# Last batch of a capped-attention and routed-experts kernel: gates of its second step from values times weights, and its output products moved into the rounds of the first choice

## The chip, the core and the metric

The kernel runs on one core of a Trainium2 chip. The metric is the device time of one execution in microseconds (us). TensorE (PE on the profile) multiplies, VectorE (DVE), ScalarE (ACT) and GpSimd (POOL) work on vectors, SyncE (SP) starts most transfers. TensorE's weight loads are listed as PEld.

## The reference

Attention with capped scores for 8 batches of 12 heads, 448 tokens and 64 columns a head; then a routed layer over all 3584 tokens. Every token goes to one of 8 experts, which take at most 448 tokens each, in the order of all logits from the largest down.

```python
scores = scale * np.matmul(q, k.transpose(0, 1, 3, 2))
scores = cap * np.tanh(scores / cap)
attn = softmax(scores)                 # per query
x = np.matmul(attn, v)                 # -> [3584, 768]
logits = x @ w_gate                    # [3584, 8]
for idx in np.argsort(-logits.flatten()):
    tok, e = divmod(int(idx), 8)
    if assigned[tok] < 0 and counts[e] < 448:
        assigned[tok] = e; counts[e] += 1
for e in range(8):
    out[assigned == e] = np.maximum(x[assigned == e] @ w1[e], 0) @ w2[e]
```

## The kernel before

**Attention.** The function `attention` runs 24 steps g, three for each batch b, four heads in each (two column blocks o by two halves h). A step computes seven blocks of scores (`qk(g,r)`, lines 143 to 166): products into the PSUM tile psS (two buffers), tanh on ScalarE, then exp on ScalarE for groups of blocks; the exp of a group is issued behind the next tanh. Weights stay unnormalised in tiles e. In the same step TensorE makes the output products of the step before, `avq(g-1,...)`, into two psA tiles, and VectorE copies them into xT (`av_out`, line 219) and adds the weights up (`esum`, line 169).

**Gates.** For each batch a PSUM tile misc[b] collects twelve products (`rnd`, line 229): sums over keys of every head (kind 's') and, from the finished xT and the gate weights, unnormalised gate values (kind 'g'). VectorE copies it (`logit_in`, line 245), TensorE transposes it (`logit`, line 251), VectorE divides gate by sum and adds the heads into the logits L1 (lines 266 to 271), and `on_logits` issues the proposals (lines 473 to 501). `turnsum` (lines 239 to 241, VectorE then GpSimd) and `inv` (line 242) make the reciprocals of the sums; `scale` (line 35) divides the turned outputs Y by them and `put` (line 32) writes them to the DRAM tile xs.

**The last batch.** The last step (23) would have its outputs too late for this. So the product of values and gate weights (V times gate) is made earlier: `vload` brings the values turned (step 16), `vgate` multiplies (step 18), `vback` transposes back into the table vgs (step 21, line 128). With it `vround` (line 134) gets step 23's sums and gates from the weights directly, without outputs. The logits of batch 7 are made in two parts: `logit(b,some=True)` with the first two steps' sums and gates, and `logit(b,part)` with those of step 23. After the attention loop come `rnd(b,0,8,8)`, the four value rounds with the first part between them, half of step 23's output products (`av(g,0,...)`), and five filler products (line 346). Half of the output products (`avs`), the two scalings of batch 6 (`held`) and the transposes of the six column blocks of batch 7's outputs (`xt`, lines 40 to 47) are handed on to the next stage.

**First choice.** `select` (lines 526 to 560) finds thresholds in 16 rounds, 5 + 6 + 5: compares on VectorE (line 539 or 541) and ScalarE (line 535), a count on TensorE (line 547), a pick on VectorE (line 551). After each count, at place B, `ffn_all` puts in filler products (`warm`), an output product (`avs`) or a transpose of outputs (`units`), by the lists UN and AN; ScalarE's copies go out at place A, before the next count. After six `xt` the tile xn is complete and goes to xs in one transfer (line 47). `finalise` turns the thresholds into a list of rows; `gather` (line 851) fetches 448 rows of xs in four pieces, TensorE transposes them (line 857), and the experts follow one after another to the end of the kernel, TensorE without gaps (lines 948 and 1010).

**Order.** PE, ACT, DVE and SP run exactly in the order of the program text; GpSimd too from `ffn_all` on. In each queue a waiting instruction holds those behind it.

## Time and profile before

| what | us |
|---|---|
| median of 3 runs (all) | 841.2 (840.28, 841.2, 841.3) |
| the profiled execution, as timed | 840.35 |
| its span | 838.5 |
| last exponential of attention ends | 298.3 |
| first turn of the first choice on TensorE | 308.81 |
| gather issued | 338.92 |

| engine | busy us | share |
|---|---|---|
| PE | 818.2 | 98% |
| DVE | 594.2 | 71% |
| ACT | 565.7 | 67% |
| POOL | 393.9 | 47% |

The profile is of one execution; times in its timelines count from the start of the span. A row of a timeline gives start, length, engine, line of the kernel, operation, output and inputs, how many instructions were merged into it, and in brackets the idle time of the engine before it with what ended that.

### The profile page before, as it was taken

The page shows a single profiled execution, that of the slowest core. Times are in us where ns is not written, and L with a number is a line of the kernel's source. Part 1 is how long each engine was busy: PE and PEld are TensorE (multiplying, and loading weights), DVE is VectorE, ACT ScalarE, POOL GpSimd, SP SyncE. Part 2 cuts the span into 40 slices and gives each one's busy share as a digit, 9 for nine tenths or more (in the row PEclk, how much of TensorE's full clock was granted, in tenths as well). Part 3 has the DMA queues.
Part 4 walks back from the last instruction along what each step waited for, and adds up shares of the span by engine and source line. Part 5 has one row for each costly group of instructions (what it writes and reads, how often), then busy time and mean ns, then how long its engine had stood idle before and what let it go on. Part 6 is the DMA issues. An engine that isn't in the chain of part 4 may idle for free.

```text
span 838.5 us, 16298 instructions
## 1 busy us (share of the span) xinstructions
PE 818.2 (98%) x5784; PEld 573.7 (68%) x5784; DVE 594.2 (71%) x1914; ACT 565.7 (67%) x747; POOL 393.9 (47%) x585
## 2 busy tenths in 40 slices
PE   7999999999999988999999999999999999999997
PEld 3333333333333336688888888888888899999997
DVE  2667899989989978877878878868768874353210
ACT  7999999999999945481683684655755845544510
POOL 7600000000000033393395695686686777887843
PEclk9999999999999999999999999999999999999999
DMA  6424364654635205733566967976968958959714
GB/s 242 132 90 133 110 166 130 191 137 155 195 110 155 52 16 133 256 112 128 183 189 217 269 212 233 312 240 196 304 214 221 309 188 236 337 189 267 241 66 131
DMA packets 115859, 155.09 MB, mean 185 GB/s; under 512 B 66818, under 2 KB 80354, under 8 KB 115778
## 3 DMA queue, kind: packets, MB, share of 16 engines
q1 hardware_dynamic: 108208, 124.73, 49.3%
q0 software_dynamic: 4832, 22.03, 7.8%
q10 hardware_dynamic: 2738, 7.31, 2.3%
q8 instruction: 45, 0.74, 0.4%
q14 instruction: 36, 0.29, 0.1%
HBM read 105.18 MB, written 40.60 MB: 174 GB/s over the span
## 4 chain that ended last, share of the span: by engine, by line
PE 90%; ACT 4%; DVE 3%; issue 1%; DMA 1%; POOL 1%; SPq 0%; POOLq 0%; DVEq 0%; ACTq 0%
PE psH L948 28%; PE psH L1010 26%; PE psS L158 13%; PE psA L198 13%; PE psM L229 3%; ACT e L159 2%; ACT e L164 1%; PE psX L783 1%; PE psS L153 1%; DVE cmpD L539 1%; POOL out_dram L968 1%; PE psM L251 1%; DVE cmpD L541 1%; PE psR L547 1%; DMA on<-yb 0%
## 5 line engine op out<-in xcount | busy, mean ns | idle before, releaser
L1010 PE MATMUL psH<-hh,w2h 128*128 128x448 f32 x720 | 199.0, 367 | 0.0
L159 ACT ACTIVATE e<-psS 128x896 f32<-128x896 f32 x168 | 145.9, 916 | 13.3 <-PE psS L158 9.2
L164 ACT ACTIVATE e<-e,bias 128x1792 f32<-128x1792 f32 (+2 forms) x74 | 147.2, 1991 | 0.8
L948 PE MATMUL psH<-xgh,w1h 128*128 128x448 f32 (+1 forms) x384 | 141.8, 369 | 0.4 <-ACT xgh L898 0.2
L158 PE MATMUL psS<-tq,tk 64*64 64x448 f32 x1248 | 135.6, 543 | 5.0 <-ACT e L159 5.0
L1010 PEld LDWEIGHTS psH<-hh,w2h 128*128 128x128 f32 x720 | 134.1, 188 | 8.7 <-DVE hh L958 0.4
L948 PE MATMUL psH<-xgh,w1l 128*128 128x448 f32 (+1 forms) x384 | 139.9, 364 | 0.0
L826 POOL TENSOR_TENSOR w1l<-w1r,w1h 128x768 fp32r<-128x768 f32 x62 | 116.4, 1878 | 49.4 <-ACT w1h L819 45.1
L948 PE MATMUL psH<-xgl,w1h 128*128 128x448 f32 (+1 forms) x384 | 135.6, 366 | 0.0
L826 POOL TENSOR_TENSOR w2l<-w2r,w2h 128x768 fp32r<-128x768 f32 x64 | 132.3, 2070 | 6.0 <-ACT w2h L819 5.9
L241 POOL COPY sm<-lgt 32x84 f32<-32x84 f32 x28 | 7.0, 249 | 258.5 <-DVE lgt L239 257.7
L198 PE MATMUL psA<-e,nv 64*64 64x448 f32 x1232 | 127.7, 536 | 0.0
L1010 PE MATMUL psH<-hh,w2l 128*128 128x448 f32 x360 | 124.3, 367 | 0.0
L158 PEld LDWEIGHTS psS<-tq,tk 64*64 64x64 f32 x1248 | 42.9, 132 | 80.0 <-issue 44.8
L198 PEld LDWEIGHTS psA<-e,nv 64*64 64x64 f32 x1232 | 47.9, 133 | 67.5 <-issue 64.9
L819 ACT ACTIVATE w2h<-w2r 128x768 fp32r<-128x768 f32 x64 | 76.6, 1209 | 0.5 <-DMA w2r<-in_moe_w_dram 0.4
L948 PEld LDWEIGHTS psH<-xgh,w1h 128*128 128x128 f32 x384 | 72.4, 189 | 6.0 <-ACT xgh L898 1.3
L948 PEld LDWEIGHTS psH<-xgh,w1l 128*128 128x128 f32 x384 | 72.2, 188 | 4.5
L948 PEld LDWEIGHTS psH<-xgl,w1h 128*128 128x128 f32 x384 | 72.2, 188 | 4.4 <-DVE xgl L910 0.2
L1010 PEld LDWEIGHTS psH<-hh,w2l 128*128 128x128 f32 x360 | 67.5, 188 | 4.3
L957 ACT ACTIVATE hh<-psH 128x448 fp32r<-128x448 f32 x56 | 30.2, 539 | 57.6 <-PE psH L948 54.7
L1014 DVE STREAM_TRANSPOSE yq<-psH 128x448 f32<-128x448 f32 x45 | 35.5, 789 | 37.8 <-PE psH L1010 37.6
(400 smaller groups left out, 1285.5 us busy)
## 6 DMA issues: line engine op xcount, KB each, us to landing
w1r<-in_moe_w_dram SPq DMA_DIRECT2D x64, 384.0 KB, 4.6
w2r<-in_moe_w_dram SPq DMA_DIRECT2D x64, 384.0 KB, 5.8
nv<-in_v_dram SPq DMA_DIRECT2D x24, 448.0 KB, 5.1
tk<-in_k_dram SPq DMA_DIRECT2D x23, 448.0 KB, 3.4
tq<-in_q_dram SPq DMA_DIRECT2D x23, 448.0 KB, 4.4
yb<-yq SPq DMA_DIRECT2D x60, 168.0 KB, 3.9
xs<-Y SPq DMA_DIRECT2D x28, 336.0 KB, 5.5
on<-yb SPq DMA_DIRECT2D x7, 1152.0 KB, 7.8
```

Source lines behind the costliest of these rows:

```text
L153: for c in range(2): nc.tensor.matmul(ps[c*64:c*64+64,h,:S],tks[g,0][hp,o,u*128+c*64:u*128+c*64+64],tks[g,1][hp,o,:],start=True,stop=True)
L158: nc.tensor.matmul(ps[w:w+64,h,:S],tks[g,0][hp,o,r*64:r*64+64],tks[g,1][hp,o,:],start=True,stop=True)
L159: nc.scalar.activation(ev(g,r),ps[:,:,:S],AF.Tanh,scale=sr[0])
L164: act=lambda: nc.scalar.activation(e,e,AF.Exp,scale=sr[1],bias=bias)
L198: for h in range(2): nc.tensor.matmul(avp[g,o][h*64:h*64+64,:S],z[w,r,h,:],ev(g,r)[w,h,:],start=r==0,stop=r==6)
L229: nc.tensor.matmul(ps[k*32:k*32+32,c],lhs,rhs[:,c],start=x<4 and i==0,stop=c.stop==S and x==max(y for y in range(end) if R[y][0]==k))
L819: nc.scalar.activation(view(h),r,AF.Copy)
L826: (eng or nc.gpsimd).tensor_tensor(view(l),r,view(h).bitcast(F32),op=ALU.subtract)
L948: nc.tensor.matmul(ps[:,o:C],a[:,c,:],b[:,c,o:],start=(m==0 and o==0),stop=(m==DC*3-1)); m+=1
L957: nc.scalar.activation(h,ps[:,:C],AF.Relu)
L1010: nc.tensor.matmul(ps[:,:C],spl[p,2,hf,f//2][w][:,f%2,cc*128:cc*128+128],h[a][:,f],start=(m==0),stop=(m==nm-1))
L1014: turnq.append((now[0]+5,now[0]+(5 if p==E-1 else TL),lambda: nc.vector.transpose(yq[p][:,:,hf,cc::3],ps[:,:C])))
```

## The change

Step 22 is treated as step 23 was: its sums and gates come from values times weights as well (`vround(0,j)` within step 23, with its own tables vgs[0], wgd[0]; `vround(1,j)` is the old one). Its sums on VectorE (`esum`), its products in the loop (`avq`) and its copies (`av_out`) go. `vload`, `vgate` and `vback` run twice, at steps 10/12/13 and 15/18/19. The last step ends after its second score block and is written out: value rounds of step 22 between the score blocks, then sums and gates of batch 7's first step (`rnd(b,0,4)`), batch 6's logits, the first part of batch 7's logits between the value rounds of step 23, batch 6's `turnsum` and `inv` behind that part, its two `scale` on GpSimd and `put` behind the second copy. The output products: half of step 22's stand beside the last logits (`av(N-2,0,...)`), the other half and all of step 23's (`avlast`) go into the rounds of the first choice; the list ITEMS says for each round whether an output product ("a"), a transpose of outputs ("x") or filler is issued. The five filler products go. The PSUM pool of the outputs (psA, pT) becomes a pool psX that lives on into the experts.

```diff
-    whole=lambda g: 0<g<N-1
+    whole=lambda g: 0<g<N-2
...
-                        nc.vector.tensor_copy(vgs[w,j,2*q:2*q+2,16:24],v4[w,q].rearrange("p (h e) -> p h e",h=2))
-        def vround(j):
-            if j==0: misc[B]=pM.tile([128,512],F32,name="psM")
+                        nc.vector.tensor_copy(vgs[i][w,j,2*q:2*q+2,VW[i]:VW[i]+8],v4[w,q].rearrange("p (h e) -> p h e",h=2))
+        def vround(i,j):
+            t=misc[B-1+i]
             for o in range(2):
                 for h in range(2):
                     l=2*o+h
-                    nc.tensor.matmul(misc[B][32*l:32*l+32,:S],vgs[:,j,l,:],ev(N-1,2*j+o if j<3 else 6)[:,h,:],start=j==0,stop=j==3)
+                    nc.tensor.matmul(t[32*l:32*l+32,:S],vgs[i][:,j,l,:],ev(N-2+i,2*j+o if j<3 else 6)[:,h,:],start=j==0,stop=j==3)
...
         def esum(g,what):
-            if not 0<=g<N: return
+            if not 0<=g<N-2: return
...
+        def avlast(n):
+            g=N-1
+            avq(g,*((0,0),(1,0),(2,0),(0,1),(1,1),(2,1),(3,1))[n])
+            if n==6: return lambda: [nc.scalar.activation(xT[B-1][:,2*(g%NQ)+o,:],avp[g,o][:,:S],AF.Copy) for o in range(2)]
         def av_out(g,o):
-            if not 0<=g<N: return
+            if not 0<=g<N-2: return
...
+            elif some:
+                va=ps[:CP,:].rearrange("p (j l k) -> p j l k",j=NJ,l=4)
+                r2=xp.tile([CP,NJ,4],F32,name="rg1",bufs=1)
+                nc.vector.reciprocal(r2,va[:,:,:,16])
+                rs=xp.tile([CP,NJ,2,H//6],F32,name="rg2",bufs=1)
+                for l in range(2): nc.vector.reciprocal(rs[:,:,l,:],ps[:CP,:].rearrange("p (j s k) -> p j s k",s=8,k=16)[:,:,0::7,1+2*l])
+                t=xp.tile([CP,NJ,8,E],F32,name="lt8",bufs=1)
+                nc.vector.tensor_tensor(t[:,:,4:8,:],va[:,:,:,24:32],r2.unsqueeze(3).broadcast_to([CP,NJ,4,E]),op=ALU.mult)
+                for l in range(2):
+                    nc.vector.tensor_tensor(t[:,:,2*l:2*l+2,:],va[:,:,1+l,0:16].rearrange("p j (h e) -> p j h e",e=E),rs[:,:,l,:].unsqueeze(3).broadcast_to([CP,NJ,2,E]),op=ALU.mult)
+                nc.vector.tensor_copy(r.rearrange("p j (a h) -> p j a h",h=2)[:,:,2::2,:],r2.rearrange("p j (a h) -> p j a h",h=2))
+                nc.vector.tensor_copy(r.rearrange("p j (a h) -> p j a h",h=2)[:,:,1:4:2,:],rs)
...
-            if g==N-8: vload()
-            if g==N-6: vgate()
-            if g==N-3: vback()
+            if g==N-14: vload(0)
+            if g==N-12: vgate(0)
+            if g==N-11: vback(0)
+            if g==N-9: vload(1)
+            if g==N-6: vgate(1)
+            if g==N-5: vback(1)
...
+            if last: break
...
-        g=N-1; b=B-1
-        rnd(b,0,8,8)
+        misc[b]=pT.tile([128,512],F32,name="psX")
+        vround(0,0)
+        qk(g,2)
+        vround(0,1); vround(0,2)
+        qk(g,3); qk(g,4)
+        on_turn(bb-1)
+        rnd(bb,10,12); logit_in(bb)
+        qk(g,5); qk(g,6)
+        rnd(b,0,4)
+        vround(0,3)
+        logit(bb)
         logit_in(b)
-        turnsum(b-1)
-        vround(0); vround(1)
-        part=logit(b,some=True,pool=pT)
-        vround(2); vround(3)
+        misc[B]=pM.tile([128,512],F32,name="psM")
+        vround(1,0); vround(1,1)
+        part=logit(b,some=True)
+        turnsum(bb); inv(bb)
+        vround(1,2); vround(1,3)
         lgs[b]=xp.tile([128,S],F32,name="lg",bufs=2); ps=misc.pop(B)
         nc.vector.tensor_copy(lgs[b],ps[:,:S])
-        ps=pT.tile([128,512],F32,name="psA")
-        av(g,0,3,ps,3,2)
-        inv(b-1)
+        for i in range(2): scale(bb,i,nc.gpsimd)
+        put(bb)
+        ps=pT.tile([128,512],F32,name="psX")
+        av(N-2,0,3,ps,3,2)
         logit(b,part)
-        for j in range(3): av(g,0,j,ps,3,2)
-        ps=pT.tile([128,512],F32,name="psA")
-        for _ in range(5): nc.tensor.matmul(ps[:,:128],ident,ident,start=True,stop=True)
-    avs=[lambda ps,j=j: av(N-1,1,j,ps,0,3) for j in range(4)]
-    def held(i):
-        scale(B-2,i,nc.gpsimd)
-        if i: put(B-2)
-    return [lambda pool,i=i: lambda: held(i) for i in range(2)]+[lambda pool,p=p: xt(B-1,p,pool) for p in range(NP)],avs
+        for j in range(3): av(N-2,0,j,ps,3,2)
+        ps1=pT.tile([128,512],F32,name="psX")
+    avs=[lambda j=j: av(N-2,1,j,ps1,0,3) for j in range(4)]+[lambda n=n: avlast(n) for n in range(7)]
+    return [lambda pool,p=p: xt(B-1,p,pool) for p in range(NP)],avs
...
-    N0=1; UN=[1,0,1,0,1,0,1,0,1,1]+[0]*6; AN=(1,3,5,7)
+    ITEMS=["a","a","a","a","ax","a","x","a","a","x","a","a","x","x","x"]
...
-    units(2)
+    avs.pop(0)()
     while len(res)<1:
         step()
         if rt.pos=='B':
-            warm(2 if UN[m] else 1 if m in AN else 4)
-            if m in AN:
-                put=avs.pop(0)(pa)
-                if put: late.append(put)
-            units(UN[m%len(UN)]); m+=1
+            x=ITEMS[m] if m<len(ITEMS) else ""; m+=1
+            warm({"a":1,"x":2,"":4}.get(x,0))
+            if "a" in x:
+                copy=avs.pop(0)()
+                if copy: late.append(copy)
+            if "x" in x: units(1)
```

## Rows read from the trace of the kernel before

**Rows 1.** The page: shares of the chain that ended last, by engine.
```profile
PE 90%; ACT 4%; DVE 3%; issue 1%; DMA 1%; POOL 1%; SPq 0%; POOLq 0%; DVEq 0%; ACTq 0%
```

**Rows 2.** Timeline of ScalarE behind the value products and behind the transposition back.
```profile
225.09 1.73 ACT L159 ACTIVATE e<-psS 128x896 f32<-128x896 f32 x2 [0.71 <-PE psS L158]
227.34 0.92 ACT L159 ACTIVATE e<-psS 128x896 f32<-128x896 f32 x1 [0.53 <-PE psS L158]
...
261.56 1.73 ACT L159 ACTIVATE e<-psS 128x896 f32<-128x896 f32 x2 [0.20 <-PE psS L158]
263.81 0.92 ACT L159 ACTIVATE e<-psS 128x896 f32<-128x896 f32 x1 [0.53 <-PE psS L158]
```

**Rows 3.** Timeline of ScalarE, the last exponential of attention.
```profile
297.30 1.04 ACT L164 ACTIVATE e<-e,bias 128x896 f32<-128x896 f32 x1
```

**Rows 4.** Timeline of VectorE in the tail.
```profile
293.86 0.46 DVE L266 RECIPROCAL rin<-psM 112x48 f32<-112x48 f32 x1 [0.47 <-PE psM L251]
...
297.82 0.15 DVE L501 SCALAR_TENSOR_TENSOR r_K<-r_kk,r_Ct 112x4 f32<-112x4 f16 x1
...
300.11 0.62 DVE L245 COPY lg<-psM 128x448 f32<-128x448 f32 x1 [1.06 <-PE psM L229]
300.65 0.63 DVE L239 STREAM_TRANSPOSE lgt<-lg 128x448 f32<-128x448 f32 x1
...
303.03 0.62 DVE L277 TENSOR_REDUCE lt<-lt 112x32 f32<-112x256 f32 x1
303.84 0.62 DVE L339 COPY lg<-psM 128x448 f32<-128x448 f32 x1 [0.19 <-PE psM L134]
304.38 0.67 DVE L242 RECIPROCAL sm<-sm 128x84 f32<-128x84 f32 x1
305.29 0.26 DVE L257 RECIPROCAL rg<-psM 112x16 f32<-112x16 f32 x1 [0.24 <-PE psM L251]
...
306.61 0.19 DVE L474 TENSOR_TENSOR r_P<-L,r_m 112x32 f16<-112x32 f32 x1
...
307.58 0.19 DVE L482 TENSOR_TENSOR r_VA<-r_P,r_At 112x32 f16<-112x32 f16 x1
```

**Rows 5.** Timeline of TensorE in the tail.
```profile
302.06 1.71 PE L134 MATMUL psM<-e,vgs 128*32 128x448 f32 x16
...
307.59 1.38 PE L346 MATMUL psA<-ident 128*128 128x128 f32 x10
308.81 0.21 PE L511 MATMUL psR<-r_id,r_VA 112*128 112x112 f16 x1
```

**Rows 6.** Timelines of GpSimd and VectorE: the sums' copies, the scalings, line 652 twice.
```profile
301.41 1.11 POOL L241 COPY sm<-lgt 32x84 f32<-32x84 f32 x4 [36.78 <-DVE lgt L239]
...
309.61 4.87 POOL L35 TENSOR_TENSOR Y<-Y,sm 128x1344 f32<-128x1344 f32 x2
...
333.88 0.24 DVE L652 SCALAR_TENSOR_TENSOR gteq<-r_kk,e8s,gt 112x32 f16<-112x32 f16 x1
...
734.75 2.16 DVE L652 SCALAR_TENSOR_TENSOR gteq<-r_kk,e8s,gt 112x32 f16<-112x32 f16 x1
734.77 2.10 POOL L826 TENSOR_TENSOR w2l<-w2r,w2h 128x768 fp32r<-128x768 f32 x1
```

**Rows 7.** Timeline of TensorE: the counts of four rounds of the first choice.
```profile
320.48 0.18 PE L547 MATMUL psR<-r_cd,r_bo 128*128 128x4 bf16 x1
321.81 0.18 PE L547 MATMUL psR<-r_cd,r_bo 128*128 128x4 bf16 x1
323.12 0.18 PE L547 MATMUL psR<-r_cd,r_bo 128*128 128x4 bf16 x1
...
330.88 0.18 PE L547 MATMUL psR<-r_cd,r_bo 128*128 128x4 bf16 x1
```

**Rows 8.** Timelines (SP, GpSimd, TensorE) and, second row, the transfer's time to landing.
```profile
326.29 0.30 SPq L47 DMA_DIRECT2D xs<-xn  x1
xs<-xn SPq DMA_DIRECT2D x1, 1344.0 KB, 6.2
338.92 0.99 POOL L851 DMA_INDIRECT xg<-xs,idx  x1 [11.26 <-DVE zz L704]
344.86 0.44 PE L857 MATMUL psX<-ident,xg 128*128 128x128 f32 x2
```

More of the change, by code (lines that the diff above doesn't have):

```diff
@@ L97, in gates, with vload, vgate @@
                     nc.gpsimd.tensor_copy(gw[hp,p,c:c+8],wgs[hp,p,:])
[L98 to L104 removed]
+            for i in range(2):
+                for h in range(2): nc.gpsimd.tensor_copy(wgd[i][h*64:h*64+64,:,h*E:h*E+E],wgs[h*64:h*64+64,NP-4+2*i:NP-2+2*i,:])
+        vgs=[c2.tile([128,NJ,2*HG,32],F32,name=f"vgs{i}") for i in range(2)]
+        wgd=[c2.tile([128,2,32],F32,name=f"wgd{i}") for i in range(2)]
+        VS=(16,0); VW=(24,16)
+        for i in range(2):
+            c=VS[i]
+            nc.gpsimd.memset(vgs[i],0.0)
+            nc.gpsimd.memset(vgs[i][:,0:3,:,c:c+1],1.0)
+            for o in range(2): nc.gpsimd.memset(vgs[i][64-64*o:128-64*o,3,2*o:2*o+2,c:c+1],1.0)
+            nc.gpsimd.memset(wgd[i],0.0)
         vt={}
[L106 removed]
+        def vload(i):
             vt['t']=tp.tile([128,HG,S],F32,name="tv",bufs=1)
[L108 to L109 removed]
+            nc.sync.dma_start(vt['t'].rearrange("p m s -> p (m s)"),vl[i])
+        def vgate(i):
             ps=pM.tile([128,512],F32,name="psM"); t=vt['t']
@@ L115, in vgate, with vback @@
                         for c,u,n in [(c,u,128)] if not a*jj else [(c,u-64,128)] if o==0 else [(c,u,64),(c+64,u,64)]:
-                            nc.tensor.matmul(ps[32*k:32*k+32,c:c+n],wgd[:,o,:],t[:,o,u:u+n],start=True,stop=True)
+                            nc.tensor.matmul(ps[32*k:32*k+32,c:c+n],wgd[i][:,o,:],t[:,o,u:u+n],start=True,stop=True)
             vt['g']=xp.tile([128,256],F32,name="vg",bufs=1)
             nc.vector.tensor_copy(vt['g'],ps[:,:256])
-        def vback():
+        def vback(i):
             ps=pM.tile([128,512],F32,name="psM")
@@ L192, in avq @@
             if j==0 and x==0:
-                for o in range(2): avp[g,o]=pT.tile([128,512],F32,name="psA")
+                for o in range(2): avp[g,o]=pT.tile([128,512],F32,name="psX")
             if whole(g):
@@ L228, in rnd @@
                     else: lhs=ones[:,m,n,:]; rhs=es_t[b*NQ+m][:,n,:]
-                    nc.tensor.matmul(ps[k*32:k*32+32,c],lhs,rhs[:,c],start=x<4 and i==0,stop=c.stop==S and x==max(y for y in range(end) if R[y][0]==k))
+                    nc.tensor.matmul(ps[k*32:k*32+32,c],lhs,rhs[:,c],start=x<4 and i==0 and b<B-1,stop=b<B-1 and c.stop==S and x==max(y for y in range(end) if R[y][0]==k))
         lgs={}; lgt={}
@@ L773, in ffn_all, with warm @@
     first_rows=wp.tile([16,E],F32,name="frow",bufs=1)
-    N0=1; UN=[1,0,1,0,1,0,1,0,1,1]+[0]*6; AN=(1,3,5,7)
+    ITEMS=["a","a","a","a","ax","a","x","a","a","x","a","a","x","x","x"]
     ctx.enter_context(tc.manual_schedule(engines={ET.PE,ET.Activation,ET.DVE,ET.Pool,ET.SP}))
-    pa=pt.tile([128,512],F32,name="psX")
     m=0
     wu=[None]; end=[-99]
-    def warm(n,t=None,w=1):
-        if not t:
-            if not wu[0]: wu[0]=pt.tile([128,512],F32,name="psX")
-            t=wu[0]
-        for _ in range(n): nc.tensor.matmul(t[:,:128*w].rearrange("p (w c) -> p w c",w=w),ident,ident.unsqueeze(1).broadcast_to([128,w,128]),start=True,stop=True)
+    def warm(n,w=1):
+        if not wu[0]: wu[0]=pt.tile([128,512],F32,name="psX")
+        for _ in range(n): nc.tensor.matmul(wu[0][:,:128*w].rearrange("p (w c) -> p w c",w=w),ident,ident.unsqueeze(1).broadcast_to([128,w,128]),start=True,stop=True)
     rt.warm=warm; rt.spare=lambda: wu[0]; rt.since=lambda: now[0]-end[0]; rt.place=lambda: now[0]%320
-    warm(0)
     step()
-    units(2)
+    wu[0]=rt.pm.tile([128,512],F32,name="psM")
+    avs.pop(0)()
     while len(res)<1:
@@ L1020, in ffn_all @@
     load2(0,0,tok)
-    warm(NW,None,4)
+    warm(NW,4)
     step(); step()
@@ L1128, in lay @@
     vz=w.transpose(0,2,4,3,1,5)[:,::-1].reshape(N,128,14*D)
-    ends=np.empty((2,128,14*D),v.dtype)
-    for i,g in enumerate((0,N-1)):
+    ends=np.empty((3,128,14*D),v.dtype)
+    for i,g in enumerate((0,N-2,N-1)):
         a=v.reshape(N,4,S,D)[g]
@@ L1140, in lay @@
     out=dict(x)
-    out.update(q=by(x["q"]),k=by(x["k"]),v=np.concatenate([ends[:1],vz[1:N-1],ends[1:]]),vl=by(v)[N-1],
+    out.update(q=by(x["q"]),k=by(x["k"]),v=np.concatenate([ends[:1],vz[1:N-2],ends[1:]]),vl=by(v)[N-2:],
         moe_w1=w1.reshape(E,M//128,128,F//128,128).transpose(0,3,2,1,4).reshape(E,F//128,128,M),
```

32 lines of the change are left out of this document (11 added, 21 removed).

## The prediction, made before the changed kernel was run

> **What bounds the kernel now.** I read the page first. Its chain of work that ended last lies 90% on TensorE [rows 1], and the page's slices show a granted clock of 0.9 or more throughout: whatever delays the first expert's matmuls delays the end by as much. So the question is only when those matmuls may start. Before them stand three stages, which I then read on the timelines, engine by engine, because each has another limit.
>
> Attention (to about 298 us): ScalarE has almost no gaps. It idles only where TensorE comes late with scores, and those gaps are the price of extra TensorE work there [rows 2]. The last exponential ends at 297.30+1.04 = 298.34 [rows 3].
>
> The tail (to 309 us): the last batch's logits are a VectorE-TensorE ladder. VectorE starts on batch 6's logits at 293.86, is through with their proposals at 297.97, copies the first part of batch 7's sums and gates at 300.11 and the second at 303.84, starts the last sum at 305.29 and has the proposals' keys (VA) at 307.77 [rows 4]. TensorE turns them only at 308.81, because five filler products stand ahead of it at 307.59 [rows 5].
>
> The first choice (to 339 us): 16 rounds, each a compare on VectorE and a count on TensorE; a round with filling work on TensorE takes about 1.3 us, whatever the filling [rows 7]. Then the gather of rows is issued at 338.92, the second piece's transposes start at 344.86, and expert matmuls follow [rows 8]. Batch 7's token rows are written at 326.29 and landed 6.2 us later, at 332.5: there are 6.4 us to spare before the gather [rows 8].
>
> **The change part by part.** All times are those of the profiled execution: 838.5 us of span, 840.35 us as timed. It lies at the low end of the three runs (840.28 to 841.3, median 841.2). I walk in the trace's own clock and add up shifts.
>
> (a) One more step (22) goes through values times weights. So the value products and the transposition back run twice: at steps 12, 13, 18 and 19 instead of 18 and 21. In the kernel before, ScalarE's first activation after the products waited 0.71 us for TensorE; the one after the transposition back waited 0.20 us; the waits of 0.53 us further on belong to every such step [rows 2]. ScalarE being full, a gap stays: +0.71 +0.20 for the new pair, +0.20 at step 19, -0.20 at step 21: **+0.9 us** (0.7 if step 13 and 19 hide theirs, 1.2 if step 12 is tighter). The second 448 KB load, its place on SP's queue and the extra memsets on GpSimd at the start hide behind idle time; without that cover they cost under 1 us once.
>
> (b) Removed in the last steps: step 22's sums on VectorE, its 28 output products ahead of the last sums, both copies, and the filler. TensorE's rounds and these products stop being late. What is late next is VectorE's own queue, and here the order counts. Batch 6's transposes now stand behind four sums and gates of batch 7 and one value round, 16 instructions; 16 such took 1.6 to 1.7 us [rows 5]. So VectorE starts at 293.86+1.60 = 295.46 and, with the same 4.11 us of logits and proposals, ends at 299.57. Only then comes the copy of batch 7's first part. From a copy's start to the next read of the transposes is 305.29-303.84 = 1.45 us [rows 4]: 301.02. The first part now has nine operations, one of them the 0.62 us reduction [rows 4], the others of 0.2 to 0.3 us: I take 2.2 us (1.9 to 2.6), to 303.22. Then the change adds on VectorE, ahead of the second copy, the turn of batch 6's sums (0.63 us), GpSimd's four copies of them and the reciprocal that must wait for those. From the turn's end at 301.28 to the end of the copies, 301.41+1.11 = 302.52, are 1.24 us [rows 4, 6], and the reciprocal takes 0.67. So the second copy starts at 303.22+0.63+1.24+0.67 = 305.76, against 303.84. Queued behind that waiting reciprocal are the second copy and with it every later step; before, both hid in idle time. Last sum 1.45 later, 307.21; keys 2.48 us after that (305.29 to 307.77), 309.69. The filler is gone, TensorE turns at once: **+0.9 us** (0.3 to 1.3) against 308.81.
>
> (c) Both halves of batch 6's scaling move on GpSimd from behind the last proposals to right behind that reciprocal. Each takes 2.4 us (4.87 for two) [rows 6]: 305.9 to 308.34 and on to 310.77. VectorE's first proposal operation with two inputs in SBUF (line 474) is due 1.32 us after the last sum starts (306.61-305.29) [rows 4], at 308.53: the second half has just begun. What then happens is shown at one place of this trace: the operation of line 652, two inputs in SBUF, takes 0.24 us with GpSimd idle, and 2.16 us beside a GpSimd subtraction of 2.10 us that started 20 ns later on the page [rows 6]. In the old place of the scaling VectorE only compared one SBUF input at a time. So line 474 waits for 310.77: **+2.2 us** (0 if only the other shapes block, 4.5 if both halves do). The Trainium skill, "SBUF — State Buffer", section "Who interferes with whom", says the same more widely: a VectorE operation with two SBUF inputs and a GpSimd operation that reads SBUF exclude each other for the whole instruction, and whoever is second waits. By that rule the price is certain, by the one row it is likely; the sum is the same.
>
> (d) Rounds. Ten of them carry output products instead of four. A round with products lasted 321.81-320.48 = 1.33 us, one with transposes 323.12-321.81 = 1.31 [rows 7]; the seven products of step 23 hide just as well, and the round ahead of the second copy pair may lose 0.3. **+0.2 us** (0 to 0.6). Without that cover they would cost 0.75 us each.
>
> (e) The transposes of batch 7's outputs end five rounds later: the last stands behind the count at 330.88 instead of that at 323.12 [rows 7], because its columns come from the products just moved. From that count to the issue of the write were 326.29-323.12 = 3.17 us, landing took 6.2 [rows 8]: issue 334.05, landing 340.25. The gather would be ready at 338.92 and now waits to 340.3: **+1.4 us**. SP's three weight loads for the first expert and GpSimd's gather stand behind or beside this write; no row shows such loads beside the write or the gather right behind it. If they share, the write could be later by up to 2.5 us; if the gather meets the loads instead, its pieces come up to 1 us later; nothing makes it a gain beyond the 1.4. I take **+0.3 us**, near the plain sequence, since the loads are issued over 1.5 us after the write. TensorE has no cover: it transposes the second piece as it lands [rows 8].
>
> Sum: 0.9+0.9+2.2+0.2+1.4+0.3 = +5.9 us, 840.35+5.9 = 846.2 in the profiled execution's own time. From the median it would be 847.1; I forecast **846.5**, nearer to the first, since its terms come from there.
>
> **Rivals.** (1) No blocking in (c): if line 474 gets through, the sum is +3.7, 844.0 to 844.9. For it: the trace has one place only; against it: that place is the same pair of engines and shapes. (2) The write is in time or the gather doesn't wait for it: +4.2, 844.5 to 845.4. For it: 6.2 us is from a write that met nothing; against: the walk misses by 1.4 us. (3) Slower still: loads and write share, or both halves block, +8 to +9, 849. (4) The other side: the tail is set by the last exponential and not by VectorE. Its place is the second copy. If VectorE were through with batch 6's proposals, the first part and the reciprocal by 299.4, the copy would follow the last value round (298.34 plus 0.75 and the way to VectorE), the keys would be there 1.45+2.48 later at 303.3, 5.5 us sooner than 308.81, no scaling would be in the way, and the sum would be -5.5+0.9+0.2+1.7 = -2.7: 837.7. The point from which it decides is VectorE starting batch 6's logits before about 289; in my walk they can't before 295.46, because their transposes stand behind the last scores in TensorE's order. (5) The change does what it says and nets nothing: VectorE's queue 3 us shorter than walked and (c) absent, 841 to 842.
>
> **How the numbers follow.** Forecast 0.56, rival 1 0.13, rival 2 0.07, rival 3 0.08, all slower: 0.84. Rival 4 0.08, rival 5 0.08. This kernel's runs tell 0.2%, 1.7 us, from no change. So faster 0.08, same 0.08, slower 0.84. The range reaches from 842.5 (rivals 1 and 2 together with the low ends of (b) and (d)) to 849.5 (rival 3): it leaves out rivals 4 and 5 and little at the top.
>
> **What would show it.** In the changed profile: 0.7 us more ScalarE idle at step 12; VectorE idle for about 1.2 us ahead of the reciprocal of line 242 while the last value rounds are done; a proposal operation of about 2 us beside GpSimd's scaling; the first turn near 312.7; the write of the last batch issued near 338, the gather some 6 us later, released by that transfer instead of VectorE. I am wrong if VectorE reads the last logits before 306, or if the gather is released by VectorE. A fall of the granted clock in the longer waits of TensorE would also break the sum; the trace shows none to price it.

## The result, and the profile after

The changed kernel takes 850.5 us (median of 4 runs, 849.2 to 851.2) beside 841.25 us of the kernel before on the same chip: a ratio of 1.0105, interval 1.0082 to 1.0128. It is slower, as forecast, but by 9.3 us and not by 5.3, and above the range's end of 849.5. A second set of runs of it (the first of the experiments) gave 849.4 us, ratio 1.0120 (1.0087 to 1.0152), at that end. The profiled execution has a span of 848.7 us, 10.2 more than before. Line numbers shift: the blocked operation of line 474 is now line 503, the turn of line 511 is 540, the reciprocal of line 242 is 249, the second copy of line 339 is 371, the gather of line 851 is 879, the transposes of line 857 are 885.

The page of the changed kernel, shares of the chain that ended last by engine [rows 1]: TensorE has fallen from 90% to 87%, and DMA has risen from 1% to 2%.

```profile
PE 87%; DVE 4%; ACT 4%; DMA 2%; issue 2%; POOL 1%; SPq 0%; POOLq 0%; DVEq 0%; ACTq 0%
```

Timeline of ScalarE: a step with value products (the new one), the step behind it with the transposition back, and the last step [rows 2, 3]. In brackets the idle time ahead of the instruction and its releaser.

```profile
151.41 1.73 ACT L162 ACTIVATE e<-psS 128x896 f32<-128x896 f32 x2 [0.55 <-PE psS L161]
153.66 0.92 ACT L162 ACTIVATE e<-psS 128x896 f32<-128x896 f32 x1 [0.53 <-PE psS L161]
...
163.88 1.73 ACT L162 ACTIVATE e<-psS 128x896 f32<-128x896 f32 x2 [0.16 <-PE psS L161]
166.14 0.92 ACT L162 ACTIVATE e<-psS 128x896 f32<-128x896 f32 x1 [0.53 <-PE psS L161]
...
288.38 0.92 ACT L162 ACTIVATE e<-psS 128x896 f32<-128x896 f32 x1 [0.57 <-PE psS L156]
...
297.98 1.04 ACT L167 ACTIVATE e<-e,bias 128x896 f32<-128x896 f32 x1
```

The new pair leaves gaps of 0.55 and 0.16 us where I had 0.71 and 0.20. But the waits of 0.53 us behind them are not those of every step: at the same place of an ordinary step the kernel before waits 0.29 us. And in the last step, where scores now stand behind value products, 0.57 us replace 0.30. The two lines of the kernel before:

```profile
202.34 0.92 ACT L159 ACTIVATE e<-psS 128x896 f32<-128x896 f32 x1 [0.29 <-PE psS L158]
...
287.77 0.92 ACT L159 ACTIVATE e<-psS 128x896 f32<-128x896 f32 x1 [0.30 <-PE psS L153]
```

Timeline of VectorE in the tail [rows 4]: the copy of batch 7's first part, the first read of its transposes, the reciprocal that waits for GpSimd, the second copy, the last sum, the first proposal operation with two inputs in SBUF.

```profile
300.44 0.61 DVE L252 COPY lg<-psX 128x448 f32<-128x448 f32 x1
...
302.30 0.26 DVE L271 RECIPROCAL rg<-psM 112x16 f32<-112x16 f32 x1 [1.24 <-PE psM L258]
...
305.65 0.68 DVE L249 RECIPROCAL sm<-sm 128x84 f32<-128x84 f32 x1 [1.28 <-POOL sm L248]
306.25 0.56 DVE L371 COPY lg<-psM 128x448 f32<-128x448 f32 x1
307.55 0.26 DVE L264 RECIPROCAL rg<-psM 112x16 f32<-112x16 f32 x1 [0.74 <-PE psM L258]
...
308.86 2.47 DVE L503 TENSOR_TENSOR r_P<-L,r_m 112x32 f16<-112x32 f32 x1
```

The reciprocal waits 1.28 us, and the copy stands behind it; and line 503 takes 2.47 us where line 474 took 0.19. TensorE's timeline in the same stretch [rows 5]:

```profile
301.20 1.06 PE L258 MATMUL psM<-ident,lg 128*112 128x128 f32 x4 [3.18 <-DVE lg L252]
302.19 2.90 PE L137 MATMUL psM<-e,vgs 128*32 128x448 f32 x16
...
312.36 0.22 PE L540 MATMUL psR<-r_id,r_VA 112*128 112x112 f16 x1 [2.44 <-DVE r_VA L511]
```

And GpSimd's, the copies of the sums and the scalings [rows 6]:

```profile
304.50 1.11 POOL L248 COPY sm<-lgt 32x84 f32<-32x84 f32 x4 [39.31 <-DVE lgt L246]
306.41 4.87 POOL L35 TENSOR_TENSOR Y<-Y,sm 128x1344 f32<-128x1344 f32 x2 [0.80 <-DVE sm L249]
```

The two scalings on GpSimd end at 306.41+4.87 = 311.28; the second half of that time begins where line 503 begins, and line 503 ends with it, at 311.33. The turn comes at 312.36 (forecast 312.7). What I had not walked: the value round of 16 matmuls, 1.71 us before, takes 2.90, and the four transposes ahead of it 1.06 instead of 0.65. The busy times of 3 us each (TensorE, its weight loads, VectorE, ScalarE, GpSimd), then the granted clock, show what went with it. Two windows of the changed kernel:

```profile
298.00:301.00 3.00, 0.02 (x3) 0.00 (x0) 2.90 (x20) 1.02 (x1) 0.00 (x0) 1.00 0.00 0
301.00:304.00 3.00, 2.80 (x16) 1.27 (x20) 1.76 (x11) 0.00 (x0) 0.00 (x0) 0.54 0.00 0
```

And one of the kernel before:

```profile
301.00:304.00 3.00, 3.00 (x29) 1.01 (x24) 1.85 (x5) 0.00 (x0) 0.99 (x4) 1.00 0.00 0
```

TensorE did nothing for 3 us, because the products and the filler that stood here are gone, and was then granted 0.54 of full speed over 3 us: the lower level (1.2 GHz) for most of them, the upper (2.4 GHz) for the rest. The repetition of the same kernel shows that this need not follow. There TensorE waited 3.20 us ahead of the transposes, the clock stayed at 1.00 and the value round took 1.71 us:

```profile
302.95 1.71 PE L137 MATMUL psM<-e,vgs 128*32 128x448 f32 x16
```

In the repetition the clock fell behind the next wait, of 2.08 us, to 0.57 from 307 to 310 us. From round 15 to the gather and the first pieces, TensorE first: the last count, and the transposes of the first and the second piece [rows 7, 8]:

```profile
336.24 0.18 PE L576 MATMUL psR<-r_cd,r_bo 128*128 128x4 bf16 x1
...
349.54 0.44 PE L885 MATMUL psX<-ident,xg 128*128 128x128 f32 x2 [0.94 <-DMA xg<-xs,idx]
...
351.60 0.44 PE L885 MATMUL psX<-ident,xg 128*128 128x128 f32 x2 [1.30 <-DMA xg<-xs,idx]
```

SP's queue, the issue of the last write:

```profile
338.10 0.30 SPq L47 DMA_DIRECT2D xs<-xn  x1
```

That transfer in the table of issues (KB each, median us to landing):

```profile
xs<-xn SPq DMA_DIRECT2D x1, 1344.0 KB, 6.5
```

And the gather on GpSimd:

```profile
345.39 1.20 POOL L879 DMA_INDIRECT xg<-xs,idx  x1 [5.89 <-DVE r_m L502]
```

The last write is issued at 338.10 (forecast near 338) and landed 6.5 us later, at 344.6. The gather follows at 345.39. The releaser named is a VectorE operation that ended at 345.27, 0.12 us earlier (5.89 us is the idle time). But the gather doesn't need it: in the kernel before the same operation starts 1.7 us after the gather has started. The two lines, first the changed kernel's, then that of the kernel before:

```profile
344.85 0.42 DVE L502 TENSOR_REDUCE r_m<-L 112x32 f32<-112x256 f32 x1
...
340.61 0.42 DVE L473 TENSOR_REDUCE r_m<-L 112x32 f32<-112x256 f32 x1
```

The write is what is left, and two runs below bear it out: with the write early the wait is gone, and with the write later still the trace names it as the releaser. TensorE then waits for the first and the second piece, which it did not before.

Summed up by stages, the two profiled executions of the changed kernel against the one of the kernel before (the first activation starts between 5.55 and 6.66 us in all traces of this study, with the arrival of the first loads; it is taken out):

| stage | predicted | first | second |
|---|---|---|---|
| start to first activation | - | -1.0 | 0.0 |
| first activation to last exponential | +0.9 | +1.7 | +1.9 |
| last exponential to first turn | +3.1 | +2.9 | +2.5 |
| turn to count of round 15 | +0.2 | +0.5 | +0.5 |
| count of round 15 to gather | +1.7 | +2.4 | +2.5 |
| gather to the first 192-column matmul | 0 | +1.7 | +0.6 |
| from there to the end | 0 | +2.1 | +0.9 |
| sum | +5.9 | +10.2 | +8.8 |

### The profile page after: what moved, and what is told of

Its sections match the earlier page's. It is cut to its first block, busy times and chain, and to the rows that moved or that the text cites. A ratio compares the mean times of both kernels' runs of the same rounds, so it can differ in the third digit from the quotient of the medians.

```text
span 848.7 us, 16317 instructions
## 1 busy us (share of the span) xinstructions
PE 820.6 (97%) x5784; PEld 570.6 (67%) x5784; DVE 589.4 (69%) x1923; ACT 567.5 (67%) x749; POOL 395.2 (47%) x592
## 4 chain that ended last, share of the span: by engine, by line
PE 87%; DVE 4%; ACT 4%; DMA 2%; issue 2%; POOL 1%; SPq 0%; POOLq 0%; DVEq 0%; ACTq 0%
PE psH L976 28%; PE psH L1038 25%; PE psS L161 13%; PE psX L201 12%; PE psM L236 3%; ACT e L162 2%; ACT e L167 1%; PE psS L156 1%; DMA xg<-xz 1%; PE psM L258 1%; POOL out_dram L996 1%; DVE cmpD L570 1%; DMA xg<-xs,idx 1%; PE psX L208 1%; PE psR L576 1%
## 5 line engine op out<-in xcount | busy, mean ns | idle before, releaser
L161 PE MATMUL psS<-tq,tk 64*64 64x448 f32 x1200 | 130.5, 543 | 5.0 <-ACT e L162 5.0
L201 PE MATMUL psX<-e,nv 64*64 64x448 f32 x1176 | 121.8, 536 | 0.0
L201 PEld LDWEIGHTS psX<-e,nv 64*64 64x64 f32 x1176 | 45.6, 133 | 64.8 <-issue 62.7
```

Source lines behind the costliest of these rows:

```text
L161: nc.tensor.matmul(ps[w:w+64,h,:S],tks[g,0][hp,o,r*64:r*64+64],tks[g,1][hp,o,:],start=True,stop=True)
L201: for h in range(2): nc.tensor.matmul(avp[g,o][h*64:h*64+64,:S],z[w,r,h,:],ev(g,r)[w,h,:],start=r==0,stop=r==6)
```

## The experiments

All are the changed kernel with an edit, except three that edit the kernel before. Times are medians; ratios are to the kernel before on the same chip, with a 95% interval. "Turn" is the time from the last exponential's end to the first choices' turn on TensorE: 10.47 us before, 13.34 in the changed kernel.

**The same again, and more filler under the gather.** No edit, and

```diff
-    WG=3; NW=7; TL=24
+    WG=3; NW=10; TL=24
```

> The changed kernel once more, as the base for the other three. If the 2.1 us that the third expert loses at its start (10.5 us behind the kernel before, after 8.35 in the first two) come from the shifted order of transfers, they are there again; if they are a chance of the transfers, that start is 8 to 9 us behind in this profile, and the total near 848.5. Otherwise 850.5.

> The changed kernel with 10 instead of 7 wide filler products between the list of rows and the gathered rows, so that TensorE waits hardly at all there. Theory (the waits of 0.94 and 1.30 us brought the granted clock to half from 352 to 356 us, which cost 1.4 us): granted clock 1.0 there, the first expert 1.4 us sooner, total 849.1. Rival (the rows come too late anyway and the slow stretch hides behind other waits): total unchanged, 850.5.

Measured: 849.4 us, 1.0120 (1.0087 to 1.0152); 849.1 us, 1.0097 (1.0080 to 1.0114). Timeline of TensorE, the first expert's second matmul in the changed kernel:

```profile
352.80 0.42 PE L902 MATMUL psH<-xgh,w1l 128*128 128x256 f32 x1
```

The same matmul with more filler:

```profile
353.27 0.28 PE L902 MATMUL psH<-xgh,w1l 128*128 128x256 f32 x1
```

And in the repetition without the edit:

```profile
353.30 0.28 PE L902 MATMUL psH<-xgh,w1l 128*128 128x256 f32 x1
```

In the first execution of the changed kernel the granted clock is 0.57 from 352 to 355 us, behind waits of 0.94 and 1.30 us for the gathered pieces; with filler in those waits it is 1.00, and the matmuls take 0.28 us again. From the second piece's transposes to the 192-column matmuls it takes 3.57 us with the filler (3.61 in the kernel before) and 5.02 without. But the repetition without the edit waits 0.70 and 1.41 us for the same pieces, its clock stays at 1.00, and it has 4.10 us there, of which a wait for the third piece takes 0.28. So the fall is worth 1.4 us in one execution and is not there in the next, the filler is not shown to be what kept the clock up, and the medians don't tell the two kernels apart.

**Scalings back behind the last proposals; then the reciprocal behind the second copy.** The first edit hands GpSimd's two scalings and the write of batch 6 to the rounds, as in the kernel before; the second kernel has both edits.

```diff
-        for i in range(2): scale(bb,i,nc.gpsimd)
-        put(bb)
...
+    def held(i):
+        scale(B-2,i,nc.gpsimd)
+        if i: put(B-2)
```

```diff
-        turnsum(bb); inv(bb)
+        turnsum(bb)
...
         nc.vector.tensor_copy(lgs[b],ps[:,:S])
+        inv(bb)
```

> Batch 6's two scalings go back behind the last batch's proposals on GpSimd (handed on to the rounds, as before the change); all else as changed. Theory (VectorE's operation with two SBUF inputs waits for GpSimd's scaling): the operation of line 503 takes 0.2 us instead of 2.47, the first turn comes at 310.1 instead of 312.4, everything behind it 2.3 us sooner, total 848.2. Rival (it waits for something else, or the later waits swallow the gain): first turn unchanged, or total within 0.5 us of the changed kernel's.

> As e_scale, and the reciprocal of batch 6's sums goes behind the second copy on VectorE. Theory (the queue of VectorE alone sets the second copy): the wait of 1.28 us and the 0.68 us of the reciprocal go from the path, a further 1.9 us, first turn at 308.2, total 846.3. Rival (TensorE's last value rounds, which ran at half the granted clock until 305.1, set it): the copy starts at 305.1 instead of 306.25, a further 1.1 us only, total 847.1.

Measured: 847.7 us, 1.0089 (1.0071 to 1.0106); 846.8 us, 1.0070 (1.0053 to 1.0086). The same operation of VectorE without the scaling beside it:

```profile
309.16 0.19 DVE L504 TENSOR_TENSOR r_P<-L,r_m 112x32 f16<-112x32 f32 x1
```

The turn comes after 10.66 us: 13.34 less 2.68 against the first execution, less 2.3 against the second (12.93). So the blocking is shown, at 1.8 to 2.3 us for the operation. Moving the reciprocal gives only 0.5 us more at the turn (10.16): the second copy starts 1.0 us sooner, for it then waits for the value round, which runs at half clock in this kernel too (16 matmuls in 3.05 us), and the reciprocal's own 0.67 us now stand between copy and last sum. That is the rival's reason, though it expected 1.1 us; the theory's 1.9 us did not come. The rest of the loss is not in the tail.

**The write.** Three kernels. The first is the changed one with eleven of the last products' fifteen on TensorE in the tail, where it waits, four in the rounds, and the last transposes in rounds 0, 2, 4, 6, 8 and 9, as in the kernel before. The other two are the kernel before with the transposes late.

```diff
+        ps=pT.tile([128,512],F32,name="psX")
+        for j in (3,0,1,2): av(N-2,0,j,ps,3,2)
         part=logit(b,some=True)
...
-        ps=pT.tile([128,512],F32,name="psX")
-        av(N-2,0,3,ps,3,2)
+        ps1=pT.tile([128,512],F32,name="psX")
+        for j in range(4): copy=av(N-2,1,j,ps1,0,3)
+        copy()
         logit(b,part)
-        for j in range(3): av(N-2,0,j,ps,3,2)
...
+        for n in range(3): avlast(n)
...
-    ITEMS=["a","a","a","a","ax","a","x","a","a","x","a","a","x","x","x"]
+    ITEMS=["x","a","x","a","x","a","x","a","x","x"]
```

```diff
-    N0=1; UN=[1,0,1,0,1,0,1,0,1,1]+[0]*6; AN=(1,3,5,7)
+    N0=1; UN=[0,0,0,0,1,0,1,0,0,1,0,0,0,1,1,1]; AN=(1,3,5,7)
```

```diff
-    N0=1; UN=[1,0,1,0,1,0,1,0,1,1]+[0]*6; AN=(1,3,5,7)
+    N0=1; UN=[0,0,0,0,1,0,1,0,0,1,0,0,1,1,1,0]; AN=(1,3,5,7)
```

> The changed kernel with its order around the last products altered: the four products of the last batch's second-to-last step, all seven of them on TensorE, and three products of the last step, stand in the tail between the last value products and the last logits (where TensorE otherwise waits), so that only four are left to the rounds; the six transposes of the last outputs get back the rounds that they have in the kernel before (0, 2, 4, 6, 8, 9). So the last batch's rows are written about five rounds (7 us) earlier. Theory: the late write holds the gather for 2.4 us of the loss, and TensorE's waits bring the granted clock down. Then from round 15's count to the gather it takes 6.7 us again (9.15 in the changed kernel), the gather is no longer the one waiting for the write, and the two-input VectorE operation beside the GpSimd scaling stays at 2 to 2.5 us; the time falls by 2.4 us for the write and by 0.3 to 1 us for clock and rounds: about 846.5 us. Rival: the stretch from the last count to the gather is longer for a reason other than the write (the ranks' own chain on VectorE and TensorE); then it stays at 9.1 us and the time at about 849 us.

> The kernel before with one part of the change alone: the six transposes of the last outputs stand in rounds 4, 6, 9, 13, 14 and 15, as in the changed kernel, instead of 0, 2, 4, 6, 8 and 9, so that the last batch's rows are written after the last round. Theory: this alone makes the gather wait for the write, and costs 2.4 us (from round 15's count to the gather 9.1 us instead of 6.7): about 843.6 us. Rival: the write is in time, or the lost wait is taken up by the transfers behind the gather; then the time stays within 0.5 us of the kernel before.

> The kernel before with the six transposes of the last outputs in rounds 4, 6, 9, 12, 13 and 14, which are the changed kernel's own (the run before this had its last three one round later, so that the write was queued behind three loads of weights). Theory: the write is issued 1.9 us behind round 15's count, ahead of the loads, and the gather starts 9.1 us behind that count instead of 6.7: about 843.6 us. Rival: the position behind or ahead of the loads makes no difference, and the time is again near 849.5 us.

Measured: 846.7 us, 1.0061 (1.0044 to 1.0078); 849.55 us, 1.0096 (1.0079 to 1.0113); 844.5 us, 1.0044 (1.0029 to 1.0060). The gather on GpSimd in the first (its idle time and releaser in brackets):

```profile
344.33 0.98 POOL L880 DMA_INDIRECT xg<-xs,idx  x1 [11.09 <-DVE zz L735]
```

SP's queue in the second:

```profile
335.20 1.49 SPq L765 DMA_DIRECT2D w1r<-in_moe_w_dram  x3
336.88 0.33 SPq L47 DMA_DIRECT2D xs<-xn  x1
```

Its gather on GpSimd:

```profile
346.21 1.02 POOL L851 DMA_INDIRECT xg<-xs,idx  x1 [10.24 <-DMA xs<-xn]
```

SP's queue in the third:

```profile
333.49 0.30 SPq L47 DMA_DIRECT2D xs<-xn  x1
336.10 2.37 SPq L765 DMA_DIRECT2D w1r<-in_moe_w_dram  x3
```

Its gather on GpSimd:

```profile
340.85 1.14 POOL L851 DMA_INDIRECT xg<-xs,idx  x1 [5.95 <-DVE r_m L473]
```

With the write early the count of round 15 is followed by the gather after 6.75 us (6.74 before, 9.15 in the changed kernel), and its releaser is the ranks again. This kernel would have gained more, had its rounds not taken 23.7 us (22.4 in the changed kernel), at a granted clock of 0.50 from 313.9 to 316.9 us: TensorE had been busy for 0.28 of the 3 us before, since the blocked operation still kept it waiting. With the write late and nothing else changed it is 9.22 us, and the time is 3.45 us worse (1.0 more than I expected). Of what is lost behind the gather little is due to the pieces: the second piece's transposes start 6.05 us behind it and 5.94 before. But TensorE waits 1.37 us ahead of them, the granted clock is 0.50 from 347 to 350 us, and from the first expert's first matmul to the 192-column matmuls it takes 3.76 us instead of 2.76. The second kernel was meant to be the third; its last three transposes stand one round later than the changed kernel's (12, 13, 14). That put the write on SP's queue behind three loads of weights: issued 5.3 us behind the count instead of 1.9, landing after 8.5 us instead of 6.6, 8.3 us worse in all. So the late write alone is worth 3.45 us here, and one round more would have more than doubled that.

**The value products alone.** The kernel before with its pair of value products made twice:

```diff
-            if g==N-8: vload()
-            if g==N-6: vgate()
-            if g==N-3: vback()
+            if g in (N-14,N-8): vload()
+            if g in (N-12,N-6): vgate()
+            if g in (N-11,N-3): vback()
```

> The kernel before with the last step's products of values and weights, and their transposes and copies, made twice: once more six steps earlier (loads, products and copies, with the same data). It does what the prediction's first term asks of the steps ahead of the tail, and nothing else of the change. Theory: ScalarE's exponentials wait for the value products in two more places, and the last exponential ends 0.6 to 0.9 us later, the time is 841.9 to 842.1 us. Rival: TensorE has room there, and the time stays that of the kernel before within 0.3 us.

Measured: 842.5 us, 1.0022 (1.0013 to 1.0031), +1.45 us. What ScalarE waited for in attention (us in total, times, longest), in the kernel before:

```profile
ACT e L159 <- PE psS L158: 9.2, 25, 0.7
ACT e L159 <- PE psS L153: 0.3, 1, 0.3
```

In this kernel:

```profile
ACT e L159 <- PE psS L158: 10.2, 27, 0.7
ACT e L159 <- PE psS L153: 0.3, 1, 0.3
```

In the changed kernel:

```profile
ACT e L162 <- PE psS L161: 10.0, 26, 0.7
ACT e L162 <- PE psS L156: 0.9, 2, 0.6
```

The waits add up to 9.5 us before, 10.5 here, 10.9 in the changed kernel; from the first activation to the last exponential it takes 1.1 us more here and 1.7 to 1.9 in the changed kernel.

**Everything together, and VectorE's order.** The first kernel joins the two edits of the tail and the one that brings the write forward. The second also changes the order on VectorE:

```diff
-                if b>=B-2: on_logits(b)
+                if b==B-1: on_logits(b)
...
-        logit(bb)
         logit_in(b)
+        logit(bb)
...
         nc.vector.tensor_copy(lgs[b],ps[:,:S])
-        inv(bb)
+        on_logits(bb); inv(bb)
```

> The changed kernel with three of its costs taken out together: the GpSimd scalings stand behind the last proposals (not beside VectorE's two-input operation), the wait for GpSimd's sums stands behind the second copy of the logits, and the order of products and transposes is that of the run that fills TensorE's waits (four products left to the rounds, transposes in rounds 0, 2, 4, 6, 8, 9). Theory: the costs are in series and add: the first two gave 846.8 us measured, the third 2.4 us for the write and 0.3 to 1 us for the clock, so about 843.7 us; from the last exponential to the turn of the first choices some 10 us, as in the kernel before, and from round 15's count to the gather 6.7 us. Rival: the write's cost overlaps with what the first two gave back, and the time stays at 845.5 to 846.8 us.

> As the run that takes the three costs out together, and besides it VectorE's order in the tail is altered: the copy of the last batch's first logits stands ahead of the logits of the batch before, and that batch's proposals stand behind the second copy of the last batch's logits. Theory: VectorE's queue behind the last exponential sets the end of the tail; with the other batch's work out of the way of the two copies the turn of the first choices comes 2 to 3 us sooner than in that run (7.5 to 8.5 us behind the last exponential instead of 10.2), and the time is 841 to 842 us. Rival: VectorE has the same work to do before the turn wherever it stands (the first choices need both batches' proposals), and the turn stays at about 10 us behind the last exponential: the time is that of the run without this order, within 0.5 us.

Measured: 842.6 us, 1.0029 (1.0016 to 1.0042); 841.7 us, 1.0009 (0.9999 to 1.0019). The costs taken out together do add: 842.6 against 846.8 us with two of them gone and 846.7 with the third. The turn in both is 10.98 us behind the last exponential, so the order gained nothing there, and that the second time lies in the expected 841 to 842 us is not the theory's doing; the second kernel tells that it is not VectorE's queue any more. The first copy on VectorE's timeline:

```profile
297.21 0.62 DVE L252 COPY lg<-psX 128x448 f32<-128x448 f32 x1 [1.57 <-PE psX L137]
```

TensorE's timeline:

```profile
299.29 3.38 PE L213 MATMUL psX<-e,nv 64*64 64x448 f32 x16
302.59 0.65 PE L258 MATMUL psM<-ident,lg 128*112 128x128 f32 x4
...
304.81 3.38 PE L213 MATMUL psX<-e,nv 128*64 128x448 f32 x16
308.12 0.65 PE L258 MATMUL psM<-ident,lg 128*112 128x128 f32 x4
```

The first copy ends at 297.83, and its transposes come at 302.59, behind four products of 3.38 us; the second copy's come at 308.12, behind four more. The products that were to hide in TensorE's waits had become the wait. In the second kernel's profiled execution the rounds also lost 1.3 us to a granted clock of 0.66 (from 315.9 to 318.9 us), behind a wait of 1.30 us at the first count; the same wait was followed by no fall in the kernel before.

**The order that follows from all this.** The sums of batch 6 are turned and inverted right behind the copy of its logits, and its scalings stand there too, ahead of any VectorE operation they could block; transposes come ahead of products on TensorE; the batch's proposals stand behind the second copy; and the last transposes stand in rounds 2, 4, 5, 7, 10 and 11, so that the write leaves early again. The second kernel also moves two small copies behind the last proposals and three products ahead of the last logits (and the transpose of round 7 to round 8).

```diff
         rnd(bb,10,12); logit_in(bb)
+        turnsum(bb); inv(bb)
+        for i in range(2): scale(bb,i,nc.gpsimd)
+        put(bb)
...
+        logit_in(b)
         logit(bb)
-        logit_in(b)
...
         part=logit(b,some=True)
         vround(1,2); vround(1,3)
...
+        on_logits(bb)
         logit(b,part)
+        ps=pT.tile([128,512],F32,name="psX")
+        for j in (3,0,1,2): av(N-2,0,j,ps,3,2)
```

```diff
-                nc.vector.tensor_copy(r.rearrange("p j (a h) -> p j a h",h=2)[:,:,1:4:2,:],rs)
+                fin.append(lambda: nc.vector.tensor_copy(r.rearrange("p j (a h) -> p j a h",h=2)[:,:,1:4:2,:],rs))
...
-        logit(b,part)
         ps=pT.tile([128,512],F32,name="psX")
-        for j in (3,0,1,2): av(N-2,0,j,ps,3,2)
+        for j in (3,0,1): av(N-2,0,j,ps,3,2)
+        logit(b,part)
+        av(N-2,0,2,ps,3,2)
```

> A rearrangement of the changed kernel by what the runs so far showed. The sums of the batch before are turned and inverted right behind the copy of its logits, and its scalings stand on GpSimd there, ahead of any two-input operation of VectorE; the copy of the last batch's first logits goes ahead of the logits of the batch before; that batch's proposals stand behind the second copy; the products stand behind the last logits on TensorE (five there, ten in the rounds), and the last transposes in rounds 2, 4, 5, 7, 10 and 11, so that the write leaves three rounds sooner than in the changed kernel. Theory: VectorE's and TensorE's order in the tail sets its end; the first choices' turn comes 7 to 8 us behind the last exponential (10.5 in the kernel before, 13.3 in the changed one), and the rest is as in the kernel before: 838 to 839.5 us. Rival: the gain at the tail is lost in the rounds (products past their cover, or a fall of the granted clock) or at the gather (a write still late); then the turn comes that early, but the time is 841 us or more.

> The rearranged kernel with two more moves: the two small copies of reciprocals, one of which took 1.39 us beside GpSimd's scaling where it takes 0.17 us alone, stand behind the first choices' last proposal; and three of the products stand on TensorE in its wait ahead of the last logits, three behind them, so that nine are left to the rounds. Theory: VectorE's queue sets the tail's end, and the copy's 1.2 us come off it: the turn comes 6.2 to 6.5 us behind the last exponential (7.6 in the run before), the rounds take 22.0 us instead of 22.6, and the time is 838.2 to 838.9 us. Rival: the operation that comes next on VectorE beside the scaling (the reduction of the first part) is held in the copy's place; then the turn stays at 7.4 us or more and the time at 839.5 us or more.

Measured: 840.2 us, 0.9990 (0.9981 to 0.9999); 838.8 us, 0.9974 (0.9963 to 0.9984), 2.3 us faster than the kernel before. The turn comes after 7.58 us in the first and 6.93 in the second (10.47 before). The first still missed its 838 to 839.5 us: attention is 1.7 us longer than in the kernel before, and from the turn to the count of round 15 it takes 24.14 us instead of 23.37. The scalings on GpSimd's timeline in the first:

```profile
296.78 4.87 POOL L35 TENSOR_TENSOR Y<-Y,sm 128x1344 f32<-128x1344 f32 x2 [0.80 <-DVE zix L802]
```

Two small copies on VectorE's timeline, the first of them beside the scalings:

```profile
300.29 1.39 DVE L278 COPY rin<-rg 112x16 f32<-112x16 f32 x1
301.60 0.16 DVE L279 COPY rin<-rg 112x16 f32<-112x16 f32 x1
```

The first of the two copies in the second kernel:

```profile
305.87 0.17 DVE L279 COPY rin<-rg 112x16 f32<-112x16 f32 x1
```

The copy of 16 columns stood from 300.29 to 301.68, until the scaling's end at 301.65, though it has one input. Put elsewhere it takes 0.17 us, and the reduction that came in its place ran beside the scaling undisturbed (0.64 us). Of the 1.2 us that it had stood, 0.65 reached the turn, since TensorE's products ahead of the last logits then held VectorE for 0.43 us. The rounds, with one product fewer, gave another 0.56 (22.06 instead of 22.62 us).

## Why the prediction was right and wrong

Right: the sign and its main cause. Rivals 4 and 5 are out: VectorE starts batch 6's logits at 296.4 and not before 289, and the tail is slower, not faster. Rival 1 is out by the runs: line 503 takes 2.0 to 2.5 us with the scaling beside it and 0.19 without. The rule of the Trainium skill, "SBUF — State Buffer", section "Who interferes with whom", that two VectorE inputs in SBUF and a GpSimd operation that reads SBUF shut each other out for the whole instruction, agrees with it. The same section says that a VectorE copy too can, under conditions, take the ports that it shares with GpSimd; the copy of 1.39 us agrees. Rival 2 is out too: with the write early the gather's wait is gone. The time is rival 3's, but not by its conditions: only one half of the scaling blocked, and the write beside the loads landed after 6.5 us instead of 6.2. The turn was forecast at 312.7 and came at 312.36 and, in the repetition, 313.14; the write's issue was forecast near 338 and came at 338.10 and 338.88. That the first execution is so near is luck: its first activation started 1.0 us earlier, and its attention took 0.8 us longer than forecast.

Wrong was the size. The steps that failed most are (a) and (e):

- (a) 0.9 us predicted, 1.7 to 1.9 measured; 1.45 by the time of the pair alone, of which its trace shows 1.1 in attention. The step that failed is "the waits of 0.53 us further on belong to every such step". An ordinary step waits 0.29 to 0.30 there, so each of the two steps costs 0.24 more; and the last step's third wait, 0.30 to 0.57, had no term at all. With the new pair's 0.55 and 0.16 that is 1.46 us; the rest of the 1.7 to 1.9 is open.
- (b) with (c), 3.1 predicted, 2.5 to 2.9 measured: right, but partly by chance. I took the value round at its 1.71 us; in the first execution it took 2.90 at half clock. That did not set the end, because the reciprocal's wait covered it; the same slow round is one reason why moving the reciprocal away gave 0.5 us and not the 1.9 of its two terms. In the repetition the four transposes behind the second copy were the slow ones (1.10 us instead of 0.65), and the blocked operation covered them: it ended with the scaling in both.
- (e) 1.7 predicted, 2.4 measured, and 3.45 in the time with the late write alone. The landing was sized nearly right (6.5 us for 6.2); the gather starts 0.8 us behind it, which no row of before could show since it never waited for this write. And the term ended at the gather, where 1.7 and 0.6 us more are lost: the filler that had covered the pieces' flight didn't move with the gather, TensorE waits 0.7 to 1.4 us for each of two pieces, and the clock fell behind these waits in the first execution. The pieces themselves come little later: the second piece's transposes start 6.05 to 6.21 us behind the gather and 5.94 before, where no wait stood ahead of them, so that rows 8 did not show them taken as the piece lands.
- (d) 0.2 predicted, 0.5 measured: inside its bounds.
- The granted clock, which I named as what would break the sum and left without a price, took 1.4 us behind the gather in the first execution and nothing there in the second, where it stayed at 1.00. The 1.2 us of the value round were covered, as said. No row of before could price it; the runs show 2.90 to 3.05 us at the lower level for a value round of 1.71, and no fall behind some waits as long.

Not settled: the last row of the table. 0.9 us of the 2.1 are also there in the three kernels that only edit the kernel before (490.9 to 491.0 us behind that matmul, against 490.0 in the one trace of it shown; all the traces lie between 489.8 and 492.1), so they need not be the change. The other 1.1 us fall at the third expert's start, where TensorE waits 1.5 us for the gathered rows' halves; in the other traces the waits of this kind are 0.2 to 1.3 us in all. What moves it wasn't tried. Nor was it settled what the gather waits for in the 0.8 us between the write's landing and its own start; the gather starts 0.8 us behind the landing in all seven traces in which it waits for the write.

## What to carry to other kernels

When work is moved off a path, price what it covered: here TensorE's late products and filler had filled waits behind which its clock fell in some executions, and GpSimd's late scaling had kept VectorE free. A transfer that gets later costs its landing, what the queue holds ahead of it and the cover that its readers had, so look at the order on the issuing queue first; one round more was worth another 5 us. Removing one cost at a time showed that the costs add up, but that only brought back the old time; the rearranged order of all the engines, with the write early, beat it by 2.3 us.

## What the runs showed of the hardware

A VectorE copy of 112x16 from SBUF to SBUF stood 1.39 us beside a GpSimd two-input operation (0.17 alone), while reductions, reciprocals and operations with an input in PSUM ran beside it at their usual times (0.64, 0.46 and 0.56 us). A VectorE operation of 112x32 with two inputs in SBUF stood 2.02 to 2.47 us beside it (0.19 alone). A write of 1344 KB issued behind three loads of 384 KB landed after 8.5 us instead of 6.6. A gather that waited for a write started 0.8 us behind its landing. The granted clock fell to 0.5 to 0.6 behind TensorE waits of 0.9 to 3.2 us in several stretches, but not behind each, and not in each execution of the same kernel.
